# Causal scores in half blocks of 64 keys, and the last check counted on TensorE

## The chip, the cores and the metric

The kernel runs on one core of a Trainium2 chip. The metric is the device time of one execution in microseconds (us). TensorE multiplies matrices, VectorE (DVE) and ScalarE (ACT) work on the results, GpSimd (POOL) and SyncE (SP) mostly start transfers.

## The reference, cut to what matters

There are 4 sequences of 768 steps, with 8 heads of size 48. A gated linear recurrence is followed by a feed-forward block with the activation h cos(h).

```
for t in range(S):                                   # S = 768
    new_re = ar * S_re - ai * S_im                   # ar, ai: gates of step t
    new_im = ar * S_im + ai * S_re
    S_re, S_im = new_re + k[t] v[t]^T, new_im
    y[t] = q[t] @ S_re
x = y as (B*S, H*D) = (3072, 384)
h = x @ w_in                                         # 384 x 2048
out = (h * cos(h)) @ w_out                           # 2048 x 384
```

## The kernel before, in words

**Chunks and groups.** The 3072 rows are cut into 24 chunks of C = 128 steps, and two chunks make one of 12 groups (g). In a chunk, the gates are folded into keys and queries of 96 numbers (real and imaginary part), so that the recurrence becomes causal attention inside the chunk plus a product with a state of 96 x 48 per head that is carried from chunk to chunk. All matmuls of interest are fp32, and the profile shows each of them as two records, two passes over the same columns.

- `f_scores(n, hh)` (L958) makes the scores of four heads of chunk n: one matmul per head, 128 keys by 128 queries, into one PSUM tile (`sc`). One VectorE multiply with `causal`, a 128x128 mask, writes them to `atm`. It is called twice a chunk, for hh = 0 and 1.
- `f_out(n)` (L970) makes the output of the chunk, transposed (`yp`). Heads go in pairs: the even head ("side" 0) is written to PSUM partitions 0 to 47, the odd one to partitions 64 to 111. For each pair there are two matmuls of the values with `atm` and two of the state with the queries. ScalarE then copies `yp` to `yT`.
- `state_sums` (L1015) makes the next state (`sp`). `f_rows` (L989) is another form of the output, for the first two chunks.
- `mm1_sums` (L1061) makes h (`hp`), `gate_sine` and `gate_product` make h cos(h) (`gate`), and `seventh` (L1160) makes the second product in seven quarter-size products (`sum`, `op`), as in Strassen's method.

**Order.** TensorE's instructions are chained in the order in which the program writes them. `weave` (L1213) mixes the lists of steps of a stage by places between 0 and 1. In the stage of group n, the scores, states and outputs (`chunks(n)`) lie between 0 and 0.36, between pieces of the second product of group n-1; then come the rest of that product and the first product of group n. Until the end of group 1 the order is written by hand. Groups 0 and 1 have their queries in another layout (`PEG` is 2, L565); groups 2 to 11 hold chunks 4 to 23.

**GpSimd's queue** fetches constants and weights. The weights come as 64-bit floats, and in the later stages they are fetched once more, two parts a stage, to look at their exponents (`guarded`, L1281). Each is behind a small copy that waits for the last gate of the group before.

**The last check.** The fast path is valid for inputs in a certain range. `verdict` (L1608) reduces what was recorded on the way (`least`, `odd`, `wide`), sends 96 + 128 numbers by two transfers to DRAM and by a third back to one partition (`line`), and takes the minimum. All engines read the flag, and a branch leads either to `general_path` or to the last store, which ScalarE starts. `seventh` arranges its last products around this with `late`, a dictionary of the instructions that others are put behind.

Of the kernel before, what the change touches and what calls it, by code (L numbers as in the profile page):

```python
# [11 lines left out]
F32 = mybir.dt.float32  # L12
# [7 lines left out]
ALU = mybir.AluOpType  # L20
# [467 lines left out]
def fast_path(ctx, tc, q, k, v, a_re, a_im, moe_w_in, moe_w_out, out, least, odd, wide,  # L488
# [7 lines left out]
    nc = tc.nc  # L496
# [46 lines left out]
    def behind(ins, other):  # L543
        tc.add_manual_dep(ins.ins, other.ins.name, mybir.DependencyInfo(
            mybir.DependencyClass.NoSync, mybir.DependencyReason.DATA))

    def constant(array, name, queue=None, pool=consts):
        t = pool.tile(list(array.shape), F32, name=name)
        put = (queue or nc.gpsimd).dma_start(
            out=t, in_=nc.inline_tensor(array, name=name + "_const").ap())  # L550
        if queue is None:
            chain(put, "gpsimd")
        return t
# [132 lines left out]
    def matmul(out, **kw):  # L686
        chain(nc.tensor.matmul(out, **kw), "tensor")  # L687
# [264 lines left out]
    def queries(n, h):  # L952
# [2 lines left out]
            return X[g]["qT"][:, i * H + h].rearrange("p q j -> p (q j)")  # L955
        return X[g]["qT"][:, :, i * H + h]

    def f_scores(n, hh):  # L958
        y = Y[n]
        if hh == 0:  # L960
            y["atm"] = ft.tile([C, H, C], F32, tag="atm", name="atm")
        ps = pa.tile([C, HH, C], F32, tag="a", name="sc")
        for h in range(HH):
            head = hh * HH + h
            matmul(ps[:, h], lhsT=X[n // G]["kT"][:, n % G * H + head],
                   rhs=queries(n, head), start=True, stop=True)
        y["masked"] = vector.tensor_tensor(
            out=y["atm"][:, ts(hh, HH)], in0=ps, in1=causal.unsqueeze(1).to_broadcast([C, HH, C]), op=ALU.mult)

    def f_out(n):  # L970
        y, (g, i) = Y[n], divmod(n, G)
        vals = X[g]["v"][:, i]
        state = y.get("state")
        if i == 0:
            X[g]["yT"] = ft.tile([C, HH, G, C], F32, tag="yT", name="yT", bufs=1)
        ps = pa.tile([C, HH, C], F32, tag="a", name="yp")
        for p in range(HH):
            for side in range(2):
                matmul(ps[ds(side * 64, D), p], lhsT=vals[:, 2 * p + side],
                       rhs=y["atm"][:, 2 * p + side], start=True, stop=(state is None))  # L980
            if state is not None:
                for side in range(2):
                    matmul(ps[ds(side * 64, D), p], lhsT=state[:, 2 * p + side],
                           rhs=queries(n, 2 * p + side), start=False, stop=True)
        for side in range(2):
            half = ds(side * 64, D)
            scalar.copy(out=X[g]["yT"][half, :, i], in_=ps[half])

    def f_rows(n, lo=0, hi=H):  # L989

        y, (g, i) = Y[n], divmod(n, G)
        state = y.get("state")
        if lo == 0:
            y["yr"] = pa.tile([C, H, D], F32, tag="a", name="yr")
        ps = y["yr"]
        for h in range(lo, hi):
            matmul(ps[:, h], lhsT=y["atm"][:, h], rhs=X[g]["v"][:, i, h],
                   start=True, stop=(state is None))
            if state is not None:
                matmul(ps[:, h], lhsT=queries(n, h), rhs=state[:, h], start=False, stop=True)  # L1000
        if hi < H:
            return
        y["rows"] = msb.tile([C, DM], F32, tag="ot", name="rows")
        scalar.copy(out=y["rows"], in_=ps.rearrange("p h d -> p (h d)"))
# [155 lines left out]
    def seventh(g, p, part):  # L1160


        x, name = X[g], SEVEN[p]
        if p == 0 and part == 0:
            x["sum"] = pm.tile([C, E2], F32, tag="acc", name="sum", bufs=1)
            x["ot"] = [msb.tile([C, DM], F32, tag="ot", name="ot") for _ in range(G)]

        alone = g == NG - 1 and p == 6
        summed = p in (0, 3, 5, 6) and not alone
        if not summed and part == 0:  # L1170
            x["op"] = pm.tile([C, E2], F32, tag="m", name="op", bufs=2)
        ps = x["sum"] if summed else x["op"]
        for j in range(part * HJ // 2, (part + 1) * HJ // 2):
            matmul(ps, lhsT=left(g, name, j), rhs=right[name][:, j],
                   start=(j == 0 and (p == 0 or not summed)),
                   stop=(j == HJ - 1), skip_group_check=summed)
        if part == 0:
            return
        c11, c12, c21, c22 = (x["ot"][i][:, ts(half, E2)] for i in range(2) for half in range(2))
        if g == NG - 1:  # L1180
            c12 = rest
        if p in (0, 3, 5) or p == 6 and not alone:
            late["scalar"] = scalar.mul(out={0: c11, 3: c21, 5: c22, 6: c12}[p], in_=ps, mul=scale)
        if g == NG - 1 and p == 5:
            scalar.mul(out=c12, in_=ps, mul=scale)
        for part_ in {1: [c11], 2: [c21], 4: [c21, c22], 6: [c12] * alone}.get(p, []):
            added = vector.scalar_tensor_tensor(out=part_, in0=ps, scalar=scale,
                                                in1=part_, op0=ALU.mult, op1=ALU.add)
            if alone:
                behind(added, late["read DVE"])  # L1190
            late["vector"] = added
        row = g * G * C
        if g == NG - 1 and p == 1:
            behind(nc.sync.dma_start(out=out[ds(row, C), 0:E2], in_=c11), late["line"])
        elif p == 4:
            put = nc.sync.dma_start(out=out[ds(row + C, C), :], in_=x["ot"][1])
            if g == NG - 1:
                behind(put, late["read SP"])
        elif p == 6 and alone:
            late["store"] = lambda: nc.scalar.dma_start(out=out[ds(row, C), E2:DM], in_=c12)  # L1200
        elif p == 6:
            nc.sync.dma_start(out=out[ds(row, C), :], in_=x["ot"][0])
# [99 lines left out]
    chain(nc.gpsimd.tensor_copy(out=alls, in_=one_b.to_broadcast([C, C])), "gpsimd")  # L1302
    parts = into + back
    pieces = [weight(dst, src) for dst, src in parts[:2]]
    causal = constant(causal_np * np.float32(0.25), "causal")
    pieces += [weight(dst, src) for dst, src in parts[2:RAW]]
    carry = constant(carry_np, "carry")
    chain(nc.gpsimd.tensor_copy(out=exact, in_=ones), "gpsimd")
# [253 lines left out]
    Ordered.by_hand, Ordered.mark = (), dict(tail)  # L1562
    for jp in 6, 7:
        mm1_gate(1, jp)
    room.close()
    stage.update(pool=ctx.enter_context(tc.tile_pool(name="late", bufs=1)), bufs=1)
    quarters()
    for n in range(2, NG):
        weave((mixes(n - 1, 2, 4), 0.0, 0.12), (logs(n + 1), 0.0, 0.02), (chunks(n), 0.0, 0.36),
              (upper[2:] if n == 2 else [], 0.0, 0.2), (products(n - 1, 0, 2 + (n < NG - 1)), 0.0, 0.36),  # L1570
              (prods(n + 1), 0.25, 0.27), (second(n - 1, 1), 0.36, 0.5),
              (products(n - 1, 2 + (n < NG - 1), 7), 0.4, 0.56),
              (phases(n + 1), *((0.472, 0.476) if n == PLAIN else (0.516, 0.524))),
              (keys(n + 1), *((0.5, 0.62) if n == PLAIN else (0.53, 0.64))),
              (last_quarter() if n == PLAIN else [], 0.9, 1.0), (first(n), 0.56, 1.0),
              (mixes(n, 0, 2), 0.9, 1.0), (guarded(n - 1, per) if n > 3 else [], 0.1, 0.9))
    checked = verdict(late, temp)

    def judged():
        late["tensor"] = tail["tensor"]  # L1580
        next(checked, None)

    weave((mixes(NG - 1, 2, 4), 0.0, 0.1), ([judged], 0.05, 0.15),
          (products(NG - 1, 0, 7), 0.0, 1.0), ([judged], 0.58, 0.6), ([judged], 0.76, 0.8))
    assert not guards
    return late
@with_exitstack
def kernel(ctx, tc, q, k, v, a_re, a_im, moe_w_in, moe_w_out, out):
# [16 lines left out]
        tc.add_manual_dep(ins.ins, other.ins.name, mybir.DependencyInfo(  # L1605
            mybir.DependencyClass.NoSync, mybir.DependencyReason.DATA))

    def verdict(late, temp):  # L1608

        low = keep.tile([D2, 1], F32, name="low")  # L1610
        nc.vector.tensor_reduce(out=low, in_=least, axis=AX.X, op=ALU.min)
# [4 lines left out]
        nc.vector.tensor_scalar(out=even, in0=even, scalar1=0.0, scalar2=None, op0=ALU.is_le)  # L1616
        nc.vector.tensor_scalar(out=most, in0=most, scalar1=2.4, scalar2=None, op0=ALU.is_le)
        nc.vector.tensor_tensor(out=even, in0=even, in1=most, op=ALU.mult)
        line_d = scratch.tile([D2 + C], F32, name="line_d")
        behind(nc.sync.dma_start(out=line_d[0:D2], in_=low.rearrange("p o -> (p o)")),  # L1620
               late["x"])
        nc.sync.dma_start(out=line_d[D2:D2 + C], in_=even.rearrange("p o -> (p o)"))
        line = temp("Q")[0:1, 0:D2 + C]
        late["line"] = nc.sync.dma_start(out=line, in_=line_d.unsqueeze(0))
        yield
        bad = keep.tile([1, 2], F32, name="bad")
        behind(nc.vector.tensor_reduce(out=bad[:, 0:1], in_=line, axis=AX.X, op=ALU.min),
               late["vector"])
        flag = keep.tile([1, 1], I32, name="flag")
        nc.vector.tensor_scalar(out=flag, in0=bad[:, 0:1], scalar1=0.5, scalar2=None,  # L1630
                                op0=ALU.is_lt)
        reads, values = nc.values_load_multi_w_load_instructions(
            flag[0:1, 0:1], min_val=0, max_val=1,
            skip_runtime_bounds_check_because="a comparison gives 0 or 1")
# [43 lines left out]
```

## Time and profile before

| | |
|---|---|
| median of 3 runs | 655.03 us (653.73 to 656.4) |
| the profiled execution | 653.01 us |
| its span, first to last instruction | 651.2 us |
| TensorE busy | 641.0 us, 98% |
| VectorE, ScalarE, GpSimd busy | 76%, 60%, 5% |
| granted TensorE clock | 1.000 |

The span is what the profile shows of one execution; 1.8 us of the profiled execution's time lie outside it. A row "PE" is a matmul record, "PEld" the load of its stationary operand, which can overlap. Shapes such as 128*48 are rows by columns of the stationary operand. A duration of one matmul is its latency; what a stream of them costs is seen from the distance of their starts, or from how long a run of them takes.

### The profile page before, as it was taken

Reading aid. Unit: us, or ns where it says so; the run is one execution under the profiler, and the core shown is the slowest. Engines: PE = TensorE matmul, PEld = TensorE weight load, DVE = VectorE, ACT = ScalarE, POOL = GpSimd, SP = SyncE. Lnnn points to the kernel's source line nnn. Section 1 sums busy time; section 2 is a strip of 40 time slices with the busy share of each in tenths; the row PEclk is TensorE's granted clock in tenths of the full one; section 3 lists DMA queues with packets and bytes.
Section 4 is the critical chain, followed back from the end, with each engine's and each line's share of the span. In section 5 each row is a group of like instructions: output and inputs, shape, how many; then the busy total and the mean of one; then the engine's idle time right before and its main releaser. Section 6 shows DMA issues by size and latency. Waiting matters only on the chain.

```text
span 651.2 us, 10758 instructions
## 1 busy us (share of the span) xinstructions
PE 641.0 (98%) x4075; PEld 576.4 (89%) x4075; DVE 492.0 (76%) x799; ACT 392.8 (60%) x726; POOL 30.9 (5%) x53
## 2 busy tenths in 40 slices
PE   8999999999999999999999999999999999999997
PEld 6888877777999999899899899899899999999996
DVE  6999989888687688786787787876877878862251
ACT  7898687284583593494494485485576476433330
POOL 4010200000000000010010010000000000000000
PEclk9999999999999999999999999999999999999999
DMA  9968755727627656747738737836836843363001
GB/s 249 244 179 203 225 164 123 170 62 182 146 49 182 158 146 148 194 110 167 209 82 191 204 85 167 205 96 151 226 105 146 219 123 98 112 134 120 25 1 31
DMA packets 232920, 94.90 MB, mean 146 GB/s; under 512 B 208701, under 2 KB 221246, under 8 KB 232858
## 3 DMA queue, kind: packets, MB, share of 16 engines
q1 hardware_dynamic: 225320, 68.51, 45.3%
q0 software_dynamic: 5824, 25.50, 11.7%
q8 instruction: 34, 0.56, 0.4%
q10 hardware_dynamic: 1714, 0.11, 0.2%
q14 instruction: 28, 0.23, 0.1%
HBM read 69.28 MB, written 24.81 MB: 144 GB/s over the span
## 4 chain that ended last, share of the span: by engine, by line
PE 92%; ACT 4%; DVE 3%; DMA 0%; issue 0%; SPq 0%; DVEq 0%
PE hp L687 38%; PE op L687 18%; PE sum L687 16%; PE sc L687 6%; PE yp L687 6%; PE sp L687 4%; PE phs L687 2%; PE lgs L687 1%; ACT tan L707 1%; PE yr L687 1%; PE tp L948 1%; ACT rs L707 1%; ACT lg L707 1%; ACT L703 1%; DVE mag L676 1%; DVE atm L676 1%
## 5 line engine op out<-in xcount | busy, mean ns | idle before, releaser
L687 PE MATMUL hp<-xT,w_in 128*128 128x256 f32 (+1 forms) x1176 | 252.5, 375 | 0.0
L687 PEld LDWEIGHTS hp<-xT,w_in 128*128 128x128 f32 x1176 | 219.6, 190 | 30.2 <-issue 0.2
L707 ACT ACTIVATE gate<-hp,half_pi_b 128x512 f32<-128x512 f32 x96 | 66.0, 687 | 118.5 <-PE hp L687 118.5
L687 PE MATMUL op<-w_out,gate 128*128 128x192 f32 (+1 forms) x448 | 100.7, 374 | 0.0
L676 DVE TENSOR_TENSOR gate<-hp,gate 128x512 f32<-128x512 f32 x96 | 65.7, 684 | 45.8 <-ACT junk L676 45.7
L687 PEld LDWEIGHTS op<-w_out,gate 128*128 128x128 f32 x448 | 75.9, 190 | 16.9 <-issue 2.0
L676 ACT ACTIVATE junk<-hp 128x512 bf16<-128x512 f32 x96 | 56.7, 591 | 0.0
L687 PE MATMUL sum<-t_s,s 128*128 128x192 f32 x320 | 56.3, 329 | 0.0
L687 PEld LDWEIGHTS sum<-t_s,s 128*128 128x128 f32 x320 | 52.1, 190 | 1.5 <-issue 1.5
L676 DVE TENSOR_TENSOR atm<-sc,causal 128x512 f32<-128x512 f32 x48 | 32.9, 689 | 23.4 <-PE sc L687 23.4
L687 PEld LDWEIGHTS sc<-qT,kT 96*128 96x128 f32 x384 | 47.4, 192 | 2.3 <-issue 0.6
L687 PE MATMUL sc<-qT,kT 96*128 96x128 f32 x384 | 49.0, 276 | 0.2 <-ACT qT L676 0.2
L676 ACT ACTIVATE ot<-sum 128x192 f32<-128x192 f32 x39 | 12.6, 322 | 53.7 <-PE sum L687 53.4
L676 DVE SCALAR_TENSOR_TENSOR ot<-op,ot 128x192 f32<-128x192 f32 x40 | 13.3, 354 | 38.0 <-PE op L687 36.4
L687 PE MATMUL yp<-atm,v 128*48 128x128 f32 x352 | 33.6, 277 | 0.9 <-ACT Q L707 0.6
L703 ACT ACT_TABLE_LOAD x24 | 30.8, 1283 | 1.2 <-PEq L1662 0.7
L676 ACT COPY yT<-yp 48x512 f32<-48x512 f32 x44 | 25.3, 574 | 7.4 <-PE yp L687 7.0
L687 PE MATMUL yp<-qT,state 96*48 96x128 f32 x304 | 29.7, 272 | 0.0
L687 PE MATMUL sum<-w_out,gate 128*128 128x192 f32 x160 | 29.7, 329 | 0.0
L687 PE MATMUL sp<-v,ks 128*96 128x48 f32 x320 | 29.7, 245 | 0.0
L687 PEld LDWEIGHTS sp<-v,ks 128*96 128x96 f32 x320 | 29.6, 165 | 0.0
L676 ACT CAST tan<-phs 128x384 int32<-128x384 f32 x24 | 11.4, 480 | 29.4 <-PE phs L687 29.4
(147 smaller groups left out, 987.4 us busy)
## 6 DMA issues: line engine op xcount, KB each, us to landing
moved<-tr SPq DMA_DIRECT2D x20, 768.0 KB
raw<-in_moe_w_in_dram POOLq DMA_DIRECT2D x16, 768.0 KB, 5.1
raw<-in_moe_w_out_dram POOLq DMA_DIRECT2D x16, 768.0 KB, 4.6
kT<-moved SPq DMA_DIRECT2D x40, 192.0 KB
qT<-moved SPq DMA_DIRECT2D x10, 768.0 KB
k<-in_k_dram SPq DMA_DIRECT2D x24, 192.0 KB
q<-in_q_dram SPq DMA_DIRECT2D x24, 192.0 KB
v<-in_v_dram SPq DMA_DIRECT2D x24, 192.0 KB
```

The source lines that it names most:

```text
L676: ins = getattr(self.engine, op)(**kw)
L687: chain(nc.tensor.matmul(out, **kw), "tensor")
L703: chain(nc.scalar.preload_act_table_set(table))
L707: chain(nc.scalar.activation(func=func, **kw))
L948: chain(nc.tensor.transpose(ps[:, h], X[g][name[0] + "s"][:, x0 + h].rearrange("p a d -> p (a d)"), ident), "tensor")
```

## The change

**Scores.** For groups from 2 on, `half_scores` takes a pair of heads at a time. Keys 0 to 63 are multiplied with all 128 queries, keys 64 to 127 with queries 64 to 127 alone. Each product has a stationary operand of 96 x 64, and the two heads of a pair write to different halves of the PSUM partitions. The result is 384 numbers per partition where there were 512, and the mask has three blocks of 64.

**Output.** `half_out` does the state first. Then the first 64 keys go with the first 64 queries: 64 rows of the array, 0 to 63 for the even head, 64 to 127 for the odd one. Then all 128 keys go with queries 64 to 127. The odd heads' scores have their two halves of keys exchanged, so `swap_values` makes a copy of the odd heads' values with the halves of the partitions exchanged (two GpSimd copies a group).

**End.** In `verdict` the three transfers and the minimum are replaced by a matmul of the 128 verdicts with ones; the flag compares the count. The last product but two of the last group is scaled twice on VectorE and no longer on ScalarE, so ScalarE reads the flag earlier. One store no longer stands behind `line`.

```
+    def swap_values(g):
+        odd_v = X[g]["odd"] = ld.tile([C, G, HH, D], F32, tag="odd", name="odd_v", bufs=1)
+        for lo in 0, C // 2:
+            src = X[g]["v"][ds(C // 2 - lo, C // 2)].rearrange("p g (x two) d -> p g x two d", two=2)
+            chain(nc.gpsimd.tensor_copy(out=odd_v[ds(lo, C // 2)], in_=src[:, :, :, 1]), "gpsimd")
+
+    def half_scores(n, hh):
+        y, (g, i), S = Y[n], divmod(n, G), C // 2
+        if hh == 0:
+            y["atm"] = ft.tile([C, HH, 3, S], F32, tag="atm", name="atm")
+        ps = pa.tile([C, HH // 2, 3, S], F32, tag="a", name="sc")
+        keys = X[g]["kT"].rearrange("d x q j -> d x (q j)")
+        for p in range(HH // 2):
+            heads = [i * H + hh * HH + 2 * p + side for side in range(2)]
+            for side, head in enumerate(heads):
+                matmul(ps[ds(side * S, S), p, ds(0, 2, 1 + side)], lhsT=keys[:, head, 0:S],
+                       rhs=X[g]["qT"][:, :, head], start=True, stop=True)
+            for side, head in (1, heads[1]), (0, heads[0]):
+                matmul(ps[ds((1 - side) * S, S), p, 1 + side], lhsT=keys[:, head, S:C],
+                       rhs=X[g]["qT"][:, Q4 // 2:Q4, head], start=True, stop=True)
+        y["masked"] = vector.tensor_tensor(
+            out=y["atm"][:, ts(hh, HH // 2)], in0=ps,
+            in1=halves_mask.unsqueeze(1).to_broadcast([C, HH // 2, 3, S]), op=ALU.mult)
+
+    def half_out(n, ps):
+        y, (g, i), S = Y[n], divmod(n, G), C // 2
+        state = y.get("state")
+        for p in range(HH):
+            vals = X[g]["v"][:, i, 2 * p], X[g]["odd"][:, i, p]
+            if state is not None:
+                for side in range(2):
+                    matmul(ps[ds(side * 64, D), p], lhsT=state[:, 2 * p + side],
+                           rhs=queries(n, 2 * p + side), start=True, stop=False,
+                           skip_group_check=True)
+            for half in range(2):
+                for side in range(2):
+                    rows = ds(0, C) if half else ds(side * S, S)
+                    matmul(ps[ds(side * 64, D), p, ts(half, S)], lhsT=vals[side][rows],
+                           rhs=y["atm"][rows, p, half * (1 + side)], start=(state is None),
+                           stop=True, skip_group_check=True)
...
     def f_scores(n, hh):
+        if n >= PEG * G:
+            return half_scores(n, hh)
...
-        if p in (0, 3, 5) or p == 6 and not alone:
+        if g == NG - 1 and p == 5:
+            for out_ in c22, c12:
+                vector.tensor_scalar(out=out_, in0=ps, scalar1=scale, scalar2=None, op0=ALU.mult)
+        elif p in (0, 3, 5) or p == 6 and not alone:
             late["scalar"] = scalar.mul(out={0: c11, 3: c21, 5: c22, 6: c12}[p], in_=ps, mul=scale)
-        if g == NG - 1 and p == 5:
-            scalar.mul(out=c12, in_=ps, mul=scale)
...
-            behind(nc.sync.dma_start(out=out[ds(row, C), 0:E2], in_=c11), late["line"])
+            nc.sync.dma_start(out=out[ds(row, C), 0:E2], in_=c11)
...
+    halves_mask = constant(halves_np, "halves_mask")
...
+              ([lambda: swap_values(n + 1)] if n + 1 < NG else [], 0.4, 0.42), (second(n - 1, 1), 0.36, 0.5),
...
+    def counted(even):
+        ps = pa.tile([1, 1], F32, tag="a", name="good")
+        matmul(ps, lhsT=even, rhs=one_b, start=True, stop=True)
+        return ps
...
-        line_d = scratch.tile([D2 + C], F32, name="line_d")
-        behind(nc.sync.dma_start(out=line_d[0:D2], in_=low.rearrange("p o -> (p o)")),
-               late["x"])
-        nc.sync.dma_start(out=line_d[D2:D2 + C], in_=even.rearrange("p o -> (p o)"))
-        line = temp("Q")[0:1, 0:D2 + C]
-        late["line"] = nc.sync.dma_start(out=line, in_=line_d.unsqueeze(0))
+        nc.vector.tensor_tensor(out=even[0:D2], in0=even[0:D2], in1=low, op=ALU.mult)
         yield
-        bad = keep.tile([1, 2], F32, name="bad")
-        behind(nc.vector.tensor_reduce(out=bad[:, 0:1], in_=line, axis=AX.X, op=ALU.min),
-               late["vector"])
+        good = counted(even)
         flag = keep.tile([1, 1], I32, name="flag")
-        nc.vector.tensor_scalar(out=flag, in0=bad[:, 0:1], scalar1=0.5, scalar2=None,
-                                op0=ALU.is_lt)
+        behind(nc.vector.tensor_scalar(out=flag, in0=good, scalar1=C - 0.5, scalar2=None,
+                                       op0=ALU.is_lt), late["vector"])
```

The calls to `verdict` move with it: the step that makes the count and the flag stands at 0.42 to 0.44 of the last products instead of 0.58 to 0.6. For the first four chunks, the scores of hh = 0 and 1 are now two tiles, and `causal` lies in a pool that ends with group 1.

More of the change, by code (lines that the diff above doesn't have):

```diff
@@ L958, in f_scores @@
     def f_scores(n, hh):
+        if n >= PEG * G:
+            return half_scores(n, hh)
         y = Y[n]
-        if hh == 0:
-            y["atm"] = ft.tile([C, H, C], F32, tag="atm", name="atm")
+        pool = stage["pool"] if hh else ft
+        atm = pool.tile([C, HH, C], F32, tag="atm", name="atm", bufs=2)
+        y.setdefault("atm", []).append(atm)
         ps = pa.tile([C, HH, C], F32, tag="a", name="sc")
@@ L967, in f_scores @@
         y["masked"] = vector.tensor_tensor(
-            out=y["atm"][:, ts(hh, HH)], in0=ps, in1=causal.unsqueeze(1).to_broadcast([C, HH, C]), op=ALU.mult)
+            out=atm, in0=ps, in1=causal.unsqueeze(1).to_broadcast([C, HH, C]), op=ALU.mult)
     def f_out(n):
@@ L976, in f_out @@
         ps = pa.tile([C, HH, C], F32, tag="a", name="yp")
-        for p in range(HH):
+        if g >= PEG:
+            half_out(n, ps)
+        for p in range(HH if g < PEG else 0):
             for side in range(2):
                 matmul(ps[ds(side * 64, D), p], lhsT=vals[:, 2 * p + side],
-                       rhs=y["atm"][:, 2 * p + side], start=True, stop=(state is None))
+                       rhs=y["atm"][p // 2][:, p % 2 * 2 + side], start=True, stop=(state is None))
             if state is not None:
@@ L996, in f_rows @@
         for h in range(lo, hi):
-            matmul(ps[:, h], lhsT=y["atm"][:, h], rhs=X[g]["v"][:, i, h],
+            matmul(ps[:, h], lhsT=y["atm"][h // HH][:, h % HH], rhs=X[g]["v"][:, i, h],
                    start=True, stop=(state is None))
@@ L1304, in fast_path @@
     pieces = [weight(dst, src) for dst, src in parts[:2]]
-    causal = constant(causal_np * np.float32(0.25), "causal")
+    causal = constant(causal_np * np.float32(0.25), "causal", pool=stage["pool"])
+    S = C // 2
+    halves_np = np.stack([np.tile(causal_np[:S, :S], (2, 1)), causal_np[:, S:],
+                          np.roll(causal_np[:, S:], S, axis=0)], axis=1) * np.float32(0.25)
+    halves_mask = constant(halves_np, "halves_mask")
     pieces += [weight(dst, src) for dst, src in parts[2:RAW]]
@@ L1564, in fast_path @@
         mm1_gate(1, jp)
+    swap_values(PEG)
     room.close()
@@ L1570, in fast_path @@
               (upper[2:] if n == 2 else [], 0.0, 0.2), (products(n - 1, 0, 2 + (n < NG - 1)), 0.0, 0.36),
-              (prods(n + 1), 0.25, 0.27), (second(n - 1, 1), 0.36, 0.5),
+              (prods(n + 1), 0.25, 0.27),
+              ([lambda: swap_values(n + 1)] if n + 1 < NG else [], 0.4, 0.42), (second(n - 1, 1), 0.36, 0.5),
               (products(n - 1, 2 + (n < NG - 1), 7), 0.4, 0.56),
@@ L1576, in fast_path @@
               (mixes(n, 0, 2), 0.9, 1.0), (guarded(n - 1, per) if n > 3 else [], 0.1, 0.9))
-    checked = verdict(late, temp)
+    def counted(even):
+        ps = pa.tile([1, 1], F32, tag="a", name="good")
+        matmul(ps, lhsT=even, rhs=one_b, start=True, stop=True)
+        return ps
+    checked = verdict(late, counted)
     def judged():
@@ L1583, in fast_path @@
     weave((mixes(NG - 1, 2, 4), 0.0, 0.1), ([judged], 0.05, 0.15),
-          (products(NG - 1, 0, 7), 0.0, 1.0), ([judged], 0.58, 0.6), ([judged], 0.76, 0.8))
+          (products(NG - 1, 0, 7), 0.0, 1.0), ([judged], 0.42, 0.44), ([judged], 0.76, 0.8))
     assert not guards
@@ L1606, in behind, with verdict @@
             mybir.DependencyClass.NoSync, mybir.DependencyReason.DATA))
-    def verdict(late, temp):
+    def verdict(late, counted):
         low = keep.tile([D2, 1], F32, name="low")
```

## Prediction

> **What bounds the kernel now.** I read the page's busy times first, then the chain of work that ended last, then TensorE's waits, and last the timeline of TensorE around the two steps that change.
>
> ```profile
> PE 641.0 (98%) x4075; PEld 576.4 (89%) x4075; DVE 492.0 (76%) x799; ACT 392.8 (60%) x726; POOL 30.9 (5%) x53
> PEclk9999999999999999999999999999999999999999
> PE 92%; ACT 4%; DVE 3%; DMA 0%; issue 0%; SPq 0%; DVEq 0%
> ```
>
> TensorE is busy for 641.0 of 651.2 us, and 92% of the chain is TensorE, at a clock that never drops. The waits of TensorE (longest 1.5 us) sum to 5.1 us. So a microsecond put into TensorE's stream is a microsecond of the end, and what VectorE or ScalarE save is worth nothing except at the two ends. The question is what the new matmuls cost in the stream.
>
> The next rows are from the list of matmul groups by shape (scores, output with values, output with state), and from the chain in order of time (start, length, what; a piece runs from the end of the work before it to its own end).
>
> ```profile
> L687 PE MATMUL sc<-qT,kT 96*128 96x128 f32 x384 | 49.0, 276 | 0.2 <-ACT qT L676 0.2
> L687 PE MATMUL yp<-atm,v 128*48 128x128 f32 x352 | 33.6, 277 | 0.9 <-ACT Q L707 0.6 <-DVE atm L676 0.3
> L687 PE MATMUL yp<-qT,state 96*48 96x128 f32 x304 | 29.7, 272 | 0.0
> ...
> 339.94 1.90 PE yp L687 x32
> 341.84 2.80 PE sum L687 x16
> 344.64 2.60 PE op L687 x16
> 347.24 2.60 PE sum L687 x16
> 356.09 20.72 PE hp L687 x96
> ```
>
> From these and the timeline of the same stretch I take four rates.
>
> ```profile
> 326.33 1.06 PE L687 MATMUL sc<-qT,kT 96*128 96x128 f32 x8
> 327.22 1.47 PE L687 MATMUL sum<-w_out,gate 128*128 128x192 f32 x8
> ...
> 340.79 0.39 PE L687 MATMUL yp<-atm,v 128*48 128x128 f32 x4
> 341.01 0.39 PE L687 MATMUL yp<-qT,state 96*48 96x128 f32 x4
> 341.23 0.39 PE L687 MATMUL yp<-atm,v 128*48 128x128 f32 x4
> ```
>
> (1) A score record of 128 columns takes (327.22 - 326.33)/8 = 0.111 us. (2) In yp four such records take 0.22 us: the two heads of a pair, in different column halves of the array, run at the same time, at 0.110 per pair of records, loads of their weights included. (3) A record grows with its columns: 192 take 2.60/16 = 0.1625, 256 take 20.72/96 = 0.216; by that slope, 0.00083 us a column, 64 columns take 0.056. (4) A visit of yp costs more than its stream: 16 pairs at 0.110 are 1.76 and the row says 1.90, so 0.14 goes into coming in. The sum after it takes 2.80 where the next sum takes 2.60, so 0.20 goes into going out.
>
> The timeline shows what (4) is.
>
> ```profile
> 331.94 0.33 PE L687 MATMUL sum<-w_out,gate 128*128 128x192 f32 x1
> 332.20 0.42 PE L687 MATMUL yp<-atm,v 128*48 128x128 f32 x4
> ```
>
> The last sum should have given way after 0.16 us; yp starts after 0.26. The array runs empty for 0.10, and then the load, which is otherwise hidden, lies open (48 columns at 0.00083, 0.04; 128 columns, 0.11, on the way out). No semaphore is in it, and the yp rows of the other stages in the chain say 1.90 as well.
>
> **The change part by part.** All sums are for the 20 chunks of groups 2 to 11.
>
> *Scores, stream.* Before, a call is 8 records at 0.111, 0.888. After, it is two pairs of heads, each with two passes of 128 columns and two of 64, both heads side by side as in yp: 2 x (2 x 0.110 + 2 x 0.056) = 0.664. 40 calls x 0.224 = 9.0 us less. This needs the loads of 64 columns (0.053) to run side by side too. In yp a pair's loads start 0.01 apart, so I take that; if they go one after the other, a pair of passes costs 0.11 whatever its columns, and the gain is nil.
>
> *Scores, visits.* Scores were a full-width product like their neighbours and are now 64 columns wide like yp, so each visit pays the entry and the exit: 0.10 + 64 columns of load 0.05 + 0.20 = 0.35. In the orders of the two programs' instructions on TensorE, otherwise alike, entries from full width to column halves go from 22 to 52, since scores stand as 8, 8 and 16 records between other products. 30 x 0.35 = 10.5 us more.
>
> *Output, stream.* The product with atm had, per pair of heads, two passes of 128 columns, 0.22. It now has four of 64, 0.224. Nothing changes: the quarter left out shortens the sum over keys, not the columns that stream. The number of loads doubles (48 columns, 0.04, under the 0.056 of a pass).
>
> *Output, 64 rows.* The products of the first 64 keys use 64 rows and 64 columns of the array, between products of all rows and 64 columns: two changes per pair of heads, 8 per chunk, 160 in all. No run shown has a change of rows. The nearest row is (4), the change of columns into yp: 0.14 with a 48-column load. Bounds: 0 (the array goes on), and 0.20 (the dearest change in the trace). The Trainium skill, "TensorEngine Tiling (Array Packing)", section "Key Properties", says that changing the tiling mode drains TensorE, without a size. The trace agrees for columns at 0.10. I take 0.14: 160 x 0.14 = 22.4 us more (0 to 32).
>
> The same page, "Theoretical Speedup", gives up to 2x for an output of at most 64 columns and more where both dimensions are small. By that rule alone the scores would save 9 us or more and nothing would be paid; by the rows of yp and sum the same edit costs 24 us. The trace has the price of the visit, so I go with the rows.
>
> *Masks.* 40 of the 48 multiplies (0.689 us for 512 elements) shrink to 384 elements, about 0.13 less each (256 elements take 0.42 in the timeline), 5 us of VectorE. VectorE is not in the chain here: worth 0.
>
> *swap_values.* Two GpSimd copies of 64x384 per group; the nearest row is a 128x128 cast at 0.45, so about 1 us a group on an engine that is 5% busy. They stand in its queue behind the fetches of the guard, which finish half a stage before the values are read: worth 0. If the copies were late, yp would wait with all TensorE behind it. The extra constant is one more transfer (0.55 us of issue) ahead of the weights, which wait for free buffers: worth 0, at most 0.5.
>
> *End.* SP loses three transfers, which lie beside the last products. VectorE loses a 0.38 reduction and gains a multiply and one scaling of 0.36; its idle times there are 2 to 5 us. TensorE gains one tiny matmul (`good`) between full-width products, and with it one entry and exit: about 0.35. The last store:
>
> ```profile
> 646.64 0.36 DVE L676 SCALAR_TENSOR_TENSOR rest<-op,rest 128x192 f32<-128x192 f32 x1 [2.05 <-PE op L687]
> 647.03 1.17 ACTq L1200 DMA_DIRECT2D out_dram<-rest  x1
> ```
>
> It starts 0.03 after its data: ScalarE is in its arm already. Getting there earlier gains nothing, unless the 1.17 of issue (0.34 on SP's stores) is from arriving late: 0 to 0.8 less. I take 0.2.
>
> *Sum:* -9.0 + 10.5 + 22.4 + 0.35 - 0.2 = +24. Against the profiled 653.0 that is 677.0; the median of the runs shown stands 2.0 above that execution, so 679.
>
> **The rivals.** *A change of rows is free.* Then +1.7, 656.7. For it: the trace has only changes of columns. Against: the skill's sentence, and that both change which parts of the array belong together. *Faster.* The array does not drain in the scores either, since the new loads go to a part that has finished: then only -9.0 and the end remain, 646. It decides in favour as soon as an entry and exit of the scores cost under 0.29 together and the rows nothing. Against: in the trace such a pair costs 0.34 each time. *Dearer.* Loads of small operands, or their issue, limit the stream: 64-column scores gain nothing (+9), and four 48-column loads in a row (0.08 for a pair) exceed the 0.056 pass in half_out, 0.024 x 16 x 20 = +8: 696. Against: yp's loads side by side.
>
> **How the numbers follow.** Likeliest, 0.70: 679, itself 670 to 688 (change of rows 0.09 to 0.19). Rows free, 0.12: 655 to 659. Faster, 0.06: 646. Dearer, 0.12: 688 to 705. A measurement of this kernel can tell about 0.5%, 3.3 us. The range 656 to 691 holds most of the first, most of the second and a little of the last. Faster by over 0.5% 0.06, within 0.5% 0.10, slower 0.84.
>
> **What would show it.** In the chain the row of yp grows from 1.90 to about 3.0 per chunk. The scores' 16 records (1.78) become 32 in 1.33, and the product after each has 0.20 more. Inside yp, starts lie 0.19 instead of 0.11 apart at each change to and from 64 rows. If these gaps are missing, the second rival holds; if the 64-column records stand 0.1 apart, the last. If TensorE's waits on VectorE or GpSimd grow beyond a few us, the reading of the bound is wrong.

## The result and the profile after

The changed kernel takes 705.66 us (703.46 to 707.36, 4 runs); the kernel before takes 654.38 in the same comparison. The ratio is 1.0781, 95% interval 1.0734 to 1.0828. The direction is the one forecast; the size, 51 us, is twice the forecast 24, and outside the range.

From the page of the changed kernel, busy times and the granted clock, then the shares of the chain by engine:

```profile
PE 672.7 (95%) x4717; PEld 575.9 (82%) x4717; DVE 490.1 (70%) x801; ACT 391.0 (55%) x724; POOL 49.1 (7%) x74
PEclk9999999999999999999999999999999989999999
PE 64%; DMA 16%; DVE 6%; ACT 5%; SPq 4%; issue 4%; POOL 0%; DVEq 0%; POOLq 0%; ACTq 0%
```

TensorE is busy 31.7 us more than before. But the span grew by 53.5, so 21.8 us are new idle time of TensorE (704.7 - 672.7 = 32.0, before 10.2). The chain is no longer TensorE alone: transfers have 16% of it. So two questions are to be asked apart: is the stream of matmuls as dear as forecast, and where does the idle time come from?

**The stream.** From the chain of the changed kernel, in order of time:

```profile
349.38 1.98 PE yp L687 x32
351.36 1.50 PE op L687 x8
352.86 1.49 PE sc L687 x32
354.35 1.50 PE op L687 x8
...
357.93 3.00 PE yp L687 x48
360.93 2.81 PE sum L687 x16
```

The output of a chunk was 1.90 and is 3.00, as the prediction said ("about 3.0"). The scores that stood as 16 records are 32 in 1.49: 1.33 of stream and 0.15 of entry, as summed. The product behind the output takes 2.81 (2.80 before), which is the exit. The single records inside one output, from the timeline of TensorE, show the drains:

```profile
349.40 0.22 PE L687 MATMUL yp<-atm,v 64*48 64x64 f32 x1
349.41 0.22 PE L687 MATMUL yp<-atm,odd_v 64*48 64x64 f32 x1
349.56 0.26 PE L687 MATMUL yp<-atm,v 128*48 128x64 f32 x1
349.56 0.26 PE L687 MATMUL yp<-atm,odd_v 128*48 128x64 f32 x1
349.65 0.22 PE L687 MATMUL yp<-atm,v 128*48 128x64 f32 x1
```

The two heads of a pair start 0.01 or less apart. From 64 to 128 rows 0.16 us pass between starts of passes that stream 0.056 each (0.15 from 128 to 64). The next pass follows after 0.09 and not 0.056; the profile has its load start 0.05 ahead of it, inside the pass before, so the load lies open in part. The array does drain when only the rows change. The prediction had put the whole of it, 0.19, into the first gap; it is spread over two.

**The idle time.** What TensorE waited for, longest first (engine and tile, what ended it, us in total, times, longest):

```profile
PE hp L687 <- DVE gate L676: 10.0, 5, 2.6
PE sc L687 <- DMA qT<-moved: 6.2, 4, 2.3
PE sc L687 <- issue: 2.4, 2, 1.2
```

Before, no wait for `gate` or for `qT<-moved` was in this list, and all waits of TensorE sum to 27.8 us where they were 5.1. TensorE waits at both ends of the first product: inside it for VectorE to free PSUM, and after it for the next group's queries. GpSimd's timeline of one stage of the changed kernel shows the origin:

```profile
345.56 0.36 POOL L1329 COPY after<-gate 1x1 f32<-1x1 f32 x1 [32.07 <-DVE gate L676]
361.09 1.33 POOL L963 COPY odd_v<-v 64x384 f32<-64x384 f32 x2 [15.17 <-PE yp L687]
362.37 0.75 POOL L629 DMA_DIRECT2D raw<-in_moe_w_in_dram  x1
369.86 0.76 POOL L629 DMA_DIRECT2D raw<-in_moe_w_in_dram  x1 [6.74 <-ACT ot L676]
```

And of the kernel before:

```profile
328.85 0.36 POOL L1279 COPY after<-gate 1x1 f32<-1x1 f32 x1 [38.67 <-DVE gate L676]
329.37 0.74 POOL L629 DMA_DIRECT2D raw<-in_moe_w_in_dram  x1 [0.17 <-ACT tan L749]
339.67 0.75 POOL L629 DMA_DIRECT2D raw<-in_moe_w_in_dram  x1 [9.56 <-ACT raw L676]
```

Before, the first guard fetch goes out 0.5 us after the last gate of the group before. Now it goes out 16.8 us after (362.37 - 345.56), because the copies stand in front of it and wait 15.17 us for the last output that reads the old copy (`odd_v` has one buffer). The second fetch waits for the first to be used, so it is late as well. Then VectorE, which works in order, from its timeline:

```profile
373.79 0.56 DVE L676 TENSOR_SCALAR rs<-tan 128x768 uint32<-128x768 uint32 x1
378.31 0.56 DVE L676 TENSOR_SCALAR raw<-raw 128x768 uint32<-128x768 uint32 x1 [3.96 <-DMA raw<-in_moe_w_in_dram]
378.79 0.95 DVE L676 TENSOR_TENSOR ks<-Q,lo 128x768 f32<-128x768 f32 x1
```

Its guard operation, which reads the second fetch, holds it for 3.96 us. Behind it stand the keys and queries of the next group and the gate products of this one. Before, `ks` followed `rs` with 0.24 of idle:

```profile
355.51 0.96 DVE L676 TENSOR_TENSOR ks<-Q,lo 128x768 f32<-128x768 f32 x1 [0.24 <-ACT lo L707]
```

The chain has the rest of the way, to the scores that start late:

```profile
369.86 8.43 DMA raw<-in_moe_w_in_dram
...
378.79 1.82 DVE ks L676 x2
380.61 1.74 DVE qs L676 x2
...
384.58 3.25 DMA moved<-tr
...
393.12 6.57 DMA qT<-moved
...
399.82 0.89 PE sc L687 x16
```

### The profile page after: what moved, and what is told of

Its sections match the earlier page's. It is cut to its first block, busy times and chain, and to the rows that moved or that the text cites. A ratio compares the mean times of both kernels' runs of the same rounds, so it can differ in the third digit from the quotient of the medians.

```text
span 704.7 us, 12094 instructions
## 1 busy us (share of the span) xinstructions
PE 672.7 (95%) x4717; PEld 575.9 (82%) x4717; DVE 490.1 (70%) x801; ACT 391.0 (55%) x724; POOL 49.1 (7%) x74
## 4 chain that ended last, share of the span: by engine, by line
PE 64%; DMA 16%; DVE 6%; ACT 5%; SPq 4%; issue 4%; POOL 0%; DVEq 0%; POOLq 0%; ACTq 0%
PE hp L687 22%; PE op L687 11%; PE sum L687 9%; PE yp L687 8%; PE sc L687 6%; DMA raw<-in_moe_w_out_dram 4%; PE sp L687 4%; DMA qT<-moved 4%; SPq L936 3%; DMA raw<-in_moe_w_in_dram 2%; DMA moved<-tr 2%; PE lgs L687 1%; DVE ks L676 1%; DVE qs L676 1%; SPq L584 1%
## 5 line engine op out<-in xcount | busy, mean ns | idle before, releaser
L687 PE MATMUL hp<-xT,w_in 128*128 128x256 f32 (+1 forms) x1176 | 258.5, 380 | 13.1 <-DVE gate L676 10.0
L676 DVE TENSOR_TENSOR atm<-sc,halves_mask 128x384 f32<-128x384 f32 x40 | 22.2, 555 | 48.9 <-PE sc L687 48.4
L687 PEld LDWEIGHTS sc<-qT,kT 96*64 96x64 f32 (+1 forms) x704 | 38.2, 146 | 18.4 <-issue 17.2
L687 PE MATMUL sc<-qT,kT 96*64 96x128 f32 (+2 forms) x704 | 42.9, 259 | 8.8 <-DMA qT<-moved 6.2
L676 ACT ACTIVATE raw<-raw,least_e_b 128x768 f32<-128x768 uint32 x16 | 16.2, 1011 | 57.7 <-DVE raw L676 57.6
L687 PE MATMUL yp<-atm,v 64*48 64x64 f32 (+2 forms) x352 | 47.3, 240 | 0.0
L687 PEld LDWEIGHTS yp<-atm,v 128*48 128x48 f32 (+1 forms) x352 | 27.8, 119 | 20.3 <-issue 11.9
L687 PE MATMUL yp<-atm,odd_v 64*48 64x64 f32 (+1 forms) x320 | 44.1, 236 | 0.0
L676 DVE TENSOR_SCALAR raw<-raw 128x768 uint32<-128x768 uint32 x16 | 9.0, 561 | 37.9 <-DMA raw<-in_moe_w_out_dram 23.1
L687 PE MATMUL sum<-w_out,gate 128*128 128x192 f32 x160 | 32.4, 349 | 0.0
```

Source lines behind the costliest of these rows:

```text
L676: ins = getattr(self.engine, op)(**kw)
```

## The experiments

Theory A: the time beyond the forecast comes from GpSimd's queue by this path. Theory B: the new stream costs twice what was summed. Each ratio is against the kernel before in the same comparison, whose medians lie between 655.28 and 655.95 us.

**The copies behind the fetches.**

```
-              ([lambda: swap_values(n + 1)] if n + 1 < NG else [], 0.4, 0.42), (second(n - 1, 1), 0.36, 0.5),
+              ([lambda: swap_values(n + 1)] if n + 1 < NG else [], 0.95, 0.97), (second(n - 1, 1), 0.36, 0.5),
```

> The changed kernel, with the two GpSimd copies of a group put at 0.95 of the stage instead of 0.4, so that they stand behind both guard fetches in GpSimd's queue; nothing else moves. Theory A (the time beyond the forecast comes from GpSimd's queue: the copies wait for the last product that reads the old copy, the guard fetches wait behind them, VectorE waits for those in order, and keys and queries come late): about 679 us, ratio to before 1.037, TensorE's waits back to about 5 us. Theory B (the matmul stream itself costs twice what was summed, the copies are bystanders): about 705, as the changed kernel.

Measured: 678.59 us, ratio 1.0334 (1.0297 to 1.0371). Theory A holds; TensorE's waits fall to 8.7 us, where about 5 was expected. GpSimd's timeline in this run:

```profile
339.32 0.37 POOL L1329 COPY after<-gate 1x1 f32<-1x1 f32 x1 [35.09 <-DVE gate L676]
339.85 0.75 POOL L629 DMA_DIRECT2D raw<-in_moe_w_in_dram  x1 [0.16 <-issue]
350.35 0.75 POOL L629 DMA_DIRECT2D raw<-in_moe_w_in_dram  x1 [9.74 <-ACT raw L676]
354.87 1.33 POOL L963 COPY odd_v<-v 64x384 f32<-64x384 f32 x2 [3.77 <-PE yp L687]
```

The fetch goes out 0.5 us after the gate again, and the copies come last. TensorE is busy for 664.2 of 677.3 us. One place in one queue was worth 27 us (705.66 - 678.59).

**All rows of the array.** On top of the run before:

```
-                    rows = ds(0, C) if half else ds(side * S, S)
+                    rows = ds(0, C)
```

> As the run before, but the product of the first 64 keys uses all 128 rows of the array, so that no change of rows is left (it adds the other head's scores in, so this part of the output is another sum). Theory A with 0.14 us per change of rows: 160 x 0.14 = 22 us less than the run before, about 657. Theory B: the changes cost more than that, 40 us or more less than the changed kernel. If a change of rows were free: no difference to the run before.

Measured: 659.17, ratio 1.0058 (1.0037 to 1.0078), 19 us below the run before. From its chain:

```profile
345.74 1.92 PE yp L687 x48
347.66 2.80 PE sum L687 x16
```

The same number of records takes 1.92 instead of 3.00. So eight changes of rows cost 1.08, 0.135 each; 0.14 was taken. The rival in which they are free falls. Over 160 changes it makes 21.6. The median fell by 19.4 and TensorE's busy time by 19.6 (664.2 to 644.6); a stretch near the start at a granted clock of 0.66 over 5 us takes up to 1.7 off the latter. The profiled execution stands 6 us above the median of this run, so the 13 us that TensorE waits in it (8.7 in the run before) do not stand for the median.

**The copies alone, in the kernel before.** Two odd heads of the second chunk are read from a copy of their values, not exchanged; the copies stand where the change has them.

```
+        odd_v = X[g]["odd"] = ld.tile([C, 2, D], F32, tag="odd", name="odd_v", bufs=1)
+        for lo in 0, C // 2:
+            src = X[g]["v"][ds(lo, C // 2), 1].rearrange("p (x two) d -> p x two d", two=2)
+            chain(nc.gpsimd.tensor_copy(out=odd_v[ds(lo, C // 2)], in_=src[:, 0:2, 1]), "gpsimd")
...
+                copied = side and g >= PEG and i == 1 and p < 2
+                own = X[g]["odd"][:, p] if copied else vals[:, 2 * p + side]
```

> The kernel before, with GpSimd copies in the same place of the queue as in the changed kernel (smaller ones: two odd heads of the second chunk, halves not exchanged, 64x96 each), read by the product with the values. Scores, outputs and end as before. Theory A: the queue alone costs about 26 us, 670 to 685. Theory B: 655, as before.

Measured: 680.65, ratio 1.0365 (1.0329 to 1.0402). The copies take 0.57 us a stage, and they cost 25 us, with the old matmuls and the old end. Its waits have the same two heads:

```profile
PE hp L687 <- DVE gate L676: 13.5, 7, 2.5
PE sc L687 <- DMA qT<-moved: 6.5, 6, 1.7
```

**The change without the fetches.**

```
-    guards = [src for _, src in into + back if src.dtype != F32]
+    guards = []
```

> The changed kernel without the guard fetches of the later stages and their two operations each (it leaves out the look at the weights' exponents). The copies still wait for the last reader of the old copy, but nothing stands behind them. Theory A (the hold acts only through the fetches behind the copies): about 677, TensorE's waits at 5 to 8 us. Theory A2 (the late copies themselves hold up the output): still about 700.

Measured: 679.81, ratio 1.0381 (1.0359 to 1.0404). The copies still wait for the last reader, as in the change, and start where they start in the run with the copies last (354.87):

```profile
354.82 1.34 POOL L963 COPY odd_v<-v 64x384 f32<-64x384 f32 x2 [50.67 <-PE yp L687]
```

With nothing behind them the wait costs nothing: the run takes about what the run with the copies last takes, and TensorE waits 8.7 us in both. So it is not the copies' lateness but what stands behind them. The run also leaves out the guards' own operations on VectorE and ScalarE; the run with the copies last keeps these and comes to about the same time.

**The new end alone.** The edits of `verdict`, of `seventh` and of the last products' weave, on the kernel before.

> The kernel before with the new end alone (verdict by a matmul with ones, VectorE scaling, flag read earlier). Both theories: 0.35 us more on TensorE and up to 0.8 less at the last store's issue, 653.5 to 655; the same within what can be measured.

Measured: 658.46, ratio 1.0038 (1.0028 to 1.0049), where nothing or a small gain was expected. The end itself behaves as summed. In the changed kernel the last store's issue is short now (1.17 before):

```profile
701.02 0.39 ACTq L1250 DMA_DIRECT2D out_dram<-rest  x1
```

From the last matmul's end to the end of the span there were 4.7 us, now 4.2 in this run and 4.1 in the changed kernel, and the last products take 0.3 longer with `good` among them. The 2.5 us lie elsewhere: in the profiled execution, which stands 3 us above the median of this kernel, some 5 us are lost before 121 us, in a part that the edit does not touch: a wait of 2.6 us for `xT<-x` at 89 us, and behind it a granted clock of 0.66 over 5 us. The run with the copies last has the same end and lost 1.0 there. So the loss does not come with the end as such; why it is there is open.

**Half scores, old output.** To see the scores' terms alone, VectorE writes the half scores into a full layout whose last quarter stays zero (three multiplies a call), and the output is the old one.

```
+    full = [ft.tile([C, HH, C], F32, name=f"atm{k}", bufs=1) for k in range(3)]
...
+        for side in range(2):
+            rows = ds(side * S, S)
+            vector.tensor_tensor(
+                out=pairs(t)[rows, :, side, 0:S], in0=ps[rows, :, 0],
+                in1=halves_mask[rows, 0].unsqueeze(1).to_broadcast([S, HH // 2, S]), op=ALU.mult)
+        y["masked"] = vector.tensor_tensor(
+            out=pairs(t)[:, :, :, S:C], in0=ps[:, :, 1:3],
+            in1=halves_mask[:, 1:3].unsqueeze(1).to_broadcast([C, HH // 2, 2, S]), op=ALU.mult)
```

> The kernel before with half scores as in the change, but written by VectorE into a full 128x128 layout whose last quarter stays zero, so that the output is the old one, two matmuls of 128 columns per pair of heads (no 64-row products); copies behind the fetches; the end as before. The scores stand where they stood. By the prediction's terms -9.0 + 10.5: 656 to 659, ratio 1.000 to 1.005. If the entries and exits of the scores cost nothing: 647.

Measured: 665.57, ratio 1.0176 (1.0149 to 1.0203); 7 us more than expected. Its largest waits name them:

```profile
PE yp L687 <- DVE atm L676: 3.9, 5, 2.0
PE hp L687 <- DMA xT<-x: 3.9, 3, 1.9
```

My reading, which no run isolates, is that what this construction adds on VectorE comes late for the output, and the output late for `xT`. TensorE's idle time grew by 9.4 us. It is busy 644.3 us against 641.0 before, so the stream gained nothing, as -9.0 + 10.5 = +1.5 says. The time alone would have hidden that.

**Fewer visits.** The second chunk's scores directly behind the first chunk's output, with half scores and with full ones:

```
-        for n in range(g * G, g * G + G):
-            for hh in range(2):
-                yield lambda n=n, hh=hh: f_scores(n, hh)
-            yield lambda n=n: f_state(n)
-            yield lambda n=n: f_out(n)
+        n = g * G
+        yield lambda: (f_scores(n, 0), f_scores(n, 1))
+        yield lambda: f_state(n)
+        yield lambda: (f_out(n), f_scores(n + 1, 0), f_scores(n + 1, 1))
+        yield lambda: f_state(n + 1)
+        yield lambda: f_out(n + 1)
```

> As the run before, but the scores of both halves of heads stand together, and those of the second chunk directly behind the output of the first, in the same width: 32 entries to column halves instead of 52 (22 before). By the terms -9.0 + 10 x 0.35 = -5.5: about 650, ratio 0.992, 7 us below the run before. If the visits are free: no difference to the run before. A rival: masks now come late for the products behind them and TensorE waits, 655 or more.

> The kernel before with only the order of the run before: full-width scores, together, the second chunk's behind the first chunk's output. The number of entries stays at 22. Expected 655 to 656, the same. If the order itself brings or costs something, it shows here and is not to be put down to the halves.

Measured: half scores 680.42 (ratio 1.0385, 1.0365 to 1.0404), full ones 668.84 (1.0225, 1.0194 to 1.0257). The order itself costs 13 us, and the control shows it. TensorE waits 13.1 us for `xT` there. SP's queue in the control:

```profile
360.61 0.24 SPq L835 DMA_DIRECT2D row<-lg  x1
360.89 0.81 SPq L1048 DMA_DIRECT2D x<-yT  x2
```

The outputs are ready at 351.4, but `x` stands behind `row`, which waits for gate work that in this order comes after the output. It is the same pattern in another queue. (In the kernel before `row` also goes first, but in this stage `x` follows at 347.67, and the product that needs it starts at 356.09.) In the run with half scores TensorE waits 14.6 us for `xT` and 6.4 for masks, the rival that its expectation named, and the granted clock falls to 0.987.

TensorE's busy time leaves the waits out and does tell what the visits are worth. It is 646.4 us with half scores. The clock of 0.987, against 0.999 in the run before, accounts for about 8 of them, so about 638 are left, an estimate. That is 6 less than the 644.3 of the run before, where 7 was forecast for 20 visits, and 3 less than in the kernel before, where 5.5 was.

**That pattern undone.** `f_x` and `f_xt` in the step of the second output, and the chunks in 0 to 0.34 instead of 0.36, so that `x` and `xT` should go out ahead of `row`.

> The joined half scores, with the transfers of the output (x, xT) put ahead of the gates' transfer (row) in SP's queue, by writing them in the same step as the second chunk's output and squeezing the chunks into 0 to 0.34. In the joined run before, TensorE waited 14.6 us for xT, since x stood in SP's queue behind row, and row waited for gate work that follows the output. If that is the cause: these waits fall to about 2 us and the time to 655 to 665 (the stream's gain of 3 to 5 us, less what the product with the masks waits for). If not: 680 as before.

> The same order with full-width scores and the old copies-free output, the control: 655 to 660 if SP's queue was the cause of its 13 us, else 669.

Measured: 663.71 (1.0121, 1.0096 to 1.0145) and 659.43 (1.0069, 1.0048 to 1.0089): 17 and 9 us back, so SP's queue was most of it. The half scores still wait 10.5 us for `xT`, the full ones 4.6, where about 2 was expected. SP's queue of the control shows what is left:

```profile
348.72 0.83 SPq L1048 DMA_DIRECT2D x<-yT  x2
353.16 0.23 SPq L835 DMA_DIRECT2D row<-lg  x1
...
355.12 0.54 SPq L1057 DMA_DIRECT2D xT<-x  x1
```

`x` goes ahead of `row` now, but `xT`, which reads it back, still goes out behind `row`: the pattern is only half undone. What the visits saved are worth cannot be read from these times, since the waits are larger than the difference. No version tried is faster than the kernel before.

## Why the prediction was wrong

**The step that failed is swap_values.** The prediction put it so: "They stand in its queue behind the fetches of the guard, which finish half a stage before the values are read: worth 0." In the order of GpSimd's instructions they stand ahead of the fetches, after the small copy that waits for the gate. The program says so: `weave` spreads that small copy and the two fetches evenly over 0.1 to 0.9 of the stage, which is 0.23, 0.5 and 0.77, and puts the copies at 0.41. The second sentence of that step, that a late copy would hold up yp, looked at the wrong victim: yp is served; the fetches behind are not. The step asked how long the copies run (about 1 us) and not what they wait for. They wait for the last reader of the one buffer, 15 to 20 us in each of the seven stages in which fetches stand behind them, and the queue waits with them. What was put at 0 is 27 us. The two experiments on the copies alone agree: 27 us less when they are moved behind, 25 us more when smaller ones are put into the kernel before. The sign that the prediction had named for a wrong reading of the bound, waits on VectorE or GpSimd beyond a few us, came: 10.0 us for `gate`.

**The halved clock was not in the sum.** Part of these 27 us is no wait. The mean granted clock fell from 1.000 to 0.990; over 704.7 us that is 7 us. Windows around three of the waits, and one microsecond inside the first (start and end, length, busy us by engine, then the granted clock):

```profile
325.00:335.00 10.00, 7.45 (x27) 5.96 (x26) 8.78 (x13) 2.87 (x8) 0.00 (x0) 0.83 0.61 182
330.00:331.00 1.00, 1.00 (x3) 0.81 (x3) 1.00 (x2) 0.00 (x0) 0.00 (x0) 0.50 0.51 197
...
495.00:505.00 10.00, 7.45 (x27) 5.88 (x27) 8.90 (x14) 2.55 (x7) 0.00 (x0) 0.83 0.65 185
568.00:580.00 12.00, 9.68 (x67) 8.59 (x66) 4.44 (x9) 5.88 (x9) 0.36 (x1) 0.72 0.18 41
```

In the first and second stretch of 10 us, TensorE had waited 2.55 us, in the stretch of 12 us 2.32. Inside, the clock is 0.50: so 0.83 over 10 us is half speed for 3.4 us, and 0.72 over 12 us is half speed for 6.7. With the copies last (0.999) and in the kernel before (1.000) there is next to none.

**The sum, closed.** The run with the copies last tells the stream from the hold (the fetches that stand behind the waiting copies). TensorE's busy time: 641.0 before, 664.2 there, 672.7 in the changed kernel. The first step, 23.2, is the stream; the second, 8.5, comes with the hold, 7 of it by the clock. Idle time: 10.2, 13.1 and 32.0, so 18.9 come with the hold. The hold makes 8.5 + 18.9 = 27.4, the rest 23.2 + 2.9 = 26.1; together 53.5, the growth of the span.

**What held.** The stream: with the hold gone the change costs 22.6 us (678.59 against 655.95), where 24 was summed, and in the profiled executions TensorE's busy time grows by 23.2. That the median of that run falls within 1 us of the forecast 679 is partly luck: its span grew by 26.1, and waits that nobody forecast are in that. The drain between 64 and 128 rows was 0.135 for a taken 0.14. That rested on the Trainium skill's sentence, "TensorEngine Tiling (Array Packing)", "Key Properties", that changing the tiling mode drains TensorE, and no row of before showed it for rows; now one does. The entries and exits of the scores, 0.15 and 0.20, are in the chain. VectorE's saving (0.689 to 0.555 a mask) was worth nothing. Loads of small operands run side by side, so the dearer rival falls; so does the one in which changes of rows are free. At the end, the last store's issue fell by 0.8 where 0.2 was taken.

**The bound was read right and then used too far.** "TensorE 98%, waits 5.1 us" was true, but it described a schedule in which every transfer was early. Its slack was not looked at: the second fetch of a stage was used by VectorE some 5 us after its issue, so a delay of 15 could not be hidden. The range, 656 to 691, was made of the uncertainty of the stream's terms alone; a term put at 0 had no share in it.

## What to carry to other kernels

An instruction put into a queue is priced by what it waits for and by what stands behind it, not by how long it runs: read the order of that queue line by line, and ask for the last reader of each buffer that it writes. Cutting a matmul into column halves saves columns, but each change of the array's shape costs a drain and an open load, so by these figures it pays only where few visits hold much work; no run here is faster for it. Before comparing times of two variants, split each into stream, idle time and clock, for an order changed on the way can cost more than the term that is being measured.

## What the runs showed of the hardware

TensorE drains for about 0.10 us at a change of its tile shape (0.10 into yp before, 0.09 between 64 and 128 rows), for a change of columns and for one of rows alike. The next load is then not hidden: by estimate from 0.00083 us a column 0.04 us for 48 columns and 0.11 for 128, which with the drain makes roughly the 0.135 of a change of rows and the 0.20 on the way out. The cost showed no spread worth naming: 3.00 us in nearly every output of the changed kernel, 1.90 in those of before.

In the changed kernel, three waits of TensorE of 2.3 to 2.6 us were followed by half clock for 3.4 or 6.7 us, which makes them cost 1.7 to 2.4 times their length, and none of its shorter waits (up to 1.8 us) was. But the length of a wait alone does not decide it. In the run with the copies alone, two waits of 2.55 us were not followed by a lower clock, and one of 1.71 was. The first of the two and the shorter one, each with a window that starts with the wait:

```profile
321.14 9.03 PE L687 MATMUL hp<-xT,w_in 128*128 128x256 f32 x40 [2.55 <-DVE gate L676]
318.60:330.00 11.40, 8.86 (x40) 7.62 (x41) 10.05 (x16) 4.45 (x11) 0.00 (x0) 1.00 0.75 198
...
553.60 1.13 PE L687 MATMUL sc<-qT,kT 96*128 96x128 f32 x8 [1.71 <-DMA qT<-moved]
551.90:563.00 11.10, 9.40 (x80) 9.21 (x80) 6.04 (x11) 7.99 (x12) 0.36 (x1) 0.85 0.05 11
```

What else decides is not shown by these runs.
